# Output products of units 3 and 4 by the seven-for-eight scheme, with the folded weights joined in DRAM

## The chip, the cores and the metric

The kernel runs on one NeuronCore of a Trainium2 chip. The metric is device time in microseconds for one execution. The kernel before takes 518.9 us, the median of 3 runs (518.61 to 520.18). A profiled execution gives a trace of every instruction of the engines: TensorE (PE, with its weight loads as PEld), VectorE (DVE), ScalarE (ACT), GpSimd (POOL) and SyncE (SP, which issues most transfers). All times below are in us.

## The reference

Attention with a local window and block summaries over 4 sequences of 768 tokens (8 heads of 64), then two gates, their product, and two more matrices with no nonlinearity between them:

```python
def _attn_ref(q, k, v):
    B, H, S, D = q.shape                                   # 4, 8, 768, 64
    block, window = (32, 16)
    k_sum = k.reshape(B, H, nb, block, D).max(axis=3)
    v_sum = v.reshape(B, H, nb, block, D).mean(axis=3)
    ...                                                    # scores in the window, and against k_sum
    a = np.exp(scores_all); a = a / (np.sum(a, axis=-1, keepdims=True) + 1e-09)
    return np.matmul(a, np.concatenate([v, v_sum], axis=2))

def _moe_ref(x, w1, w2, w3, w_out):                        # x: 3072 x 512
    a = x @ w1                                             # 512 x 1024
    b = x @ w2
    h = a * b @ w3                                         # 1024 x 1024
    return (h @ w_out)                                     # 1024 x 512
```

Because nothing stands between `w3` and `w_out`, the kernel folds them into one matrix of 1024 x 512, called the folded weights (`wp`).

## The kernel before

**Precision.** Every network matmul is done as three matmuls on values that are split into a rounded high part and a low remainder: high by high, low by high, high by low. ACT casts the high part, DVE subtracts it from the source to get the low part (`low`, L117; `halves`, L569). Tiles with a second index of 2 hold both parts.

**Units.** The 3072 tokens are six units of 512. Units 1 and 2 go through the network in the classic way (`gate`, `project`). Units 3 and 4, and units 5 and 6, go as pairs (n = 1 and n = 2) through block products with seven for eight: both operands are cut into 2 x 2 blocks, seven block products of sums and differences of blocks replace eight, and the results are added up. One product of the gates is 24 matmuls of 128 x 512 (four lanes in four PSUM banks, six each, `lanes`, L633); the gates of a pair are 14 products. The moving operands come from `moving_x` (differences on DVE, casts on ACT, low parts on DVE); the stationary operands come from DRAM as tiles `ws` of 512 KB in a ring of six (`flow_in`). The weights' own sums and differences are formed once by `stationary` and written to DRAM (`wS` for the gates, `pS` for the output).

**Output products.** For units 5 and 6 (`project_fast`, class `Whole`) the output product `h @ wp` is in the same scheme: seven products of 24 matmuls in two lanes with two banks. For units 3 and 4 (`project_split`, class `Split`) it is ordinary: the gates' result is split at once into `hs`, and 192 matmuls `lo` multiply it with the folded weights, loaded from `pW`. The sums of the output weights (`sums_of_output`, L877) load `pW` as tiles `pl`, add the high and low part, and run after the output of units 3 and 4 is issued.

**Order.** The attention works in lumps, one for each of 24 pairs of heads and units; from lump 8 on, `lump(p)` puts the transposes of pair p-2, the scores of pair p, 18 network matmuls, the outputs of pair p-2 and then more network matmuls on TensorE, up to the bound in `UP_TO` (counted in matmul columns). TensorE's order is written out by hand. ACT and DVE follow a written order inside the attention; the remaining work of ACT, DVE, POOL and SP is placed by a planner that simulates the engines by a cost model, with a priority by place in the program and a bonus for what stands in `high_priority`; it often moves work far ahead of its place where its inputs are ready. Each engine then works strictly in that order. `tasks` is a list of background generators (`moving_x`, the sums of weights); `tend` advances the first of them one step for every four matmuls.

Of the kernel before, what the change touches and what calls it, by code (L numbers as in the profile page):

```python
# [19 lines left out]
P = 128  # L20
# [50 lines left out]
def attention_moe(ctx, tc, qG, kW, kT, vP, vW, vB, mask, w1, w2, w3T, wo, out, outT):  # L71
# [41 lines left out]
    pS = {k: [tc.dram_tile([P, 2, 2 * DH], F32, name=f"pS{k}_{c}") for c in range(NF // 4)] for k in range(2, NK - 1)}  # L113
    pW = [tc.dram_tile([P, 2, DO], F32, name=f"pW{i}") for i in range(NF)]
# [324 lines left out]
    def keep_raw(po, u, c):  # L439

        n, half = divmod(u, 2)
        if (n, half) not in raws:
            if half:
                t = sb.tile([P, NC, U], F32, name="xraw", tag="w12", bufs=8)
# [5 lines left out]
        nc.scalar.copy(raws[n, half][c], po[:, :U])  # L450

# [98 lines left out]
    FIRST_OF_GROUP, LAST_OF_GROUP = (0, 2, 4), (1, 3, 6)  # L550

    def source(k, b):


        return b[(0, 1, 0, 1, 0, 0, 1)[k]][(0, 0, 0, 1, 0, 1, 0)[k]]

    def difference(k, b):

        src = source(k, b)
        if k == 2:  # L560
            nc.vector.tensor_tensor(src, b[0][1], src, ALU.subtract)
        elif k == 3:
            nc.vector.tensor_tensor(b[0][1], src, b[0][1], ALU.subtract)
        elif k == 4:
            nc.vector.tensor_tensor(src, b[1][1], src, ALU.subtract)
        elif k == 6:
            nc.vector.tensor_tensor(src, src, b[0][0], ALU.subtract)
# [7 lines left out]
    def moving(k, b, dst):  # L575

        difference(k, b)
        yield 1
        yield from halves(source(k, b), dst)
# [10 lines left out]
    def stationary(load, to_dram, home):  # L590


        t = sb.tile([P, 2, 2, 512], F32, name="wr", tag="ring", bufs=RING)
        yield from load(t)
        a11, a12, a21, a22 = (t[:, i, j] for i in range(2) for j in range(2))
        yield 1

        def finished(k, raw):
# [7 lines left out]
            nc.sync.dma_start(to_dram(k), to.bitcast(F32))  # L606

# [17 lines left out]
    def flow_in(n):  # L625


        while flow and len(ready) < n:
            t = sb.tile([P, 2, 512], F32R, name="ws", tag="x", bufs=6)
            flow.pop(0)(t)  # L630
            ready.append(t)

    def lanes(n, weights_of, moving_of, steps, evacuated, tags, between=None):  # L633

        banks = [ps.tile([P, 512], F32, name="ln", tag=tag, bufs=bufs) for tag, bufs in tags]
        for k in range(NK):
            stationary_of = yield from weights_of(k)
            for i in range(n):
                for c in range(steps):
                    if between and c % KH == 0:  # L640
                        between(k, i * steps // KH + c // KH)
                    a, m = [stationary_of(i, c, w) for w in range(2)], moving_of(k, c)
                    terms = [(a[0], m[0]), (a[1], m[0]), (a[0], m[1])]
                    for j, (x, y) in enumerate(terms):
# [4 lines left out]
                            start=c + j == 0 and k in FIRST_OF_GROUP,  # L649
# [654 lines left out]
```

## Time and profile before

| what | before |
|---|---|
| median of 3 runs | 518.9 us |
| the profiled execution, its time and span | 523.18 and 521.4 us |
| granted TensorE clock, mean | 0.989 |
| busy: PE, DVE, ACT, POOL | 496.7, 368.4, 294.6, 44.4 us |
| moved by DMA | 142.94 MB, mean 274 GB/s |
| matmuls `lo` (output of units 3 and 4) | 192 |
| matmuls `ln<-hT` (output of units 5 and 6) | 168 |

The span is the time from the first to the last instruction; the time of the execution includes what lies around it. Busy times are sums over the span. In the groups, an entry reads: line, engine, operation, what it writes and reads with the shape, its count, its busy time in all and the mean duration of one in ns, and the idle time of the engine just before with what ended it. In the timeline an entry reads: start, duration, engine, line, operation. In the chain of waits an entry is a piece of the path that ended last: start, duration, engine and line. Consecutive operations of DVE and ACT overlap at their ends, so that a row of several is shorter than the sum of their durations.

### The profile page before, as it was taken

Reading aid. Unit: us, or ns where it says so; the run is one execution under the profiler, and the core shown is the slowest. Engines: PE = TensorE matmul, PEld = TensorE weight load, DVE = VectorE, ACT = ScalarE, POOL = GpSimd, SP = SyncE. Lnnn points to the kernel's source line nnn. Section 1 sums busy time; section 2 is a strip of 40 time slices with the busy share of each in tenths; the row PEclk is TensorE's granted clock in tenths of the full one; section 3 lists DMA queues with packets and bytes.
Section 4 is the critical chain, followed back from the end, with each engine's and each line's share of the span. In section 5 each row is a group of like instructions: output and inputs, shape, how many; then the busy total and the mean of one; then the engine's idle time right before and its main releaser. Section 6 shows DMA issues by size and latency. Waiting matters only on the chain.

```text
span 521.4 us, 10271 instructions
## 1 busy us (share of the span) xinstructions
PE 496.7 (95%) x3768; PEld 398.0 (76%) x3768; DVE 368.4 (71%) x877; ACT 294.6 (57%) x839; POOL 44.4 (9%) x78
## 2 busy tenths in 40 slices
PE   1989897999999999999999999999999999999997
PEld 0767676888877777777877778887778888888885
DVE  5989986698644978896668784598444478459982
ACT  5496874467455877778896668448134410401640
POOL 1012725201040000000000000000000000000000
PEclk9989997999999999999999999999999999999999
DMA  8995779999084876869888787666899777556652
GB/s 343 416 406 244 272 248 417 378 410 404 21 298 137 289 292 211 294 237 343 300 300 290 272 294 260 219 216 228 284 370 384 274 284 256 193 196 201 203 183 101
DMA packets 48962, 142.94 MB, mean 274 GB/s; under 512 B 5136, under 2 KB 11792, under 8 KB 46352
## 3 DMA queue, kind: packets, MB, share of 16 engines
q1 hardware_dynamic: 46608, 138.09, 73.2%
q10 hardware_dynamic: 2304, 4.20, 2.1%
q8 instruction: 30, 0.49, 0.4%
q14 instruction: 20, 0.16, 0.1%
HBM read 112.71 MB, written 29.56 MB: 273 GB/s over the span
## 4 chain that ended last, share of the span: by engine, by line
PE 82%; DVE 6%; ACT 6%; DMA 5%; issue 1%; SPq 0%; POOL 0%; POOLq 0%
PE ln L645 37%; PE mm L122 27%; PE lo L122 9%; PE po L430 4%; PE sc L352 3%; ACT sm L380 3%; DMA rows<-in_vP_dram 2%; PE tp L410 2%; DVE wf L185 2%; DMA wraw<-in_w_dram 1%; DVE w L118 1%; DMA wraw<-in_wo_dram 1%; DVE wf L182 1%; DVE sm L366 1%; ACT wf L173 1%
## 5 line engine op out<-in xcount | busy, mean ns | idle before, releaser
L645 PE MATMUL ln<-xT,ws 128*128 128x512 f32 x672 | 156.8, 392 | 0.0
L645 PEld LDWEIGHTS ln<-xT,ws 128*128 128x128 f32 x672 | 125.1, 188 | 27.3 <-issue 1.0
L122 PE MATMUL mm<-x,w 128*128 128x512 f32 x384 | 92.7, 399 | 0.8 <-ACT x L454 0.7
L122 PEld LDWEIGHTS mm<-x,w 128*128 128x128 f32 x384 | 72.3, 191 | 17.8 <-ACT x L454 0.8
L380 ACT ACTIVATE sm<-sm,mx 128x120 f32<-128x120 f32 x192 | 73.7, 387 | 11.6 <-DVE mx L366 11.6
L122 PE MATMUL mm<-w,w 128*128 128x512 f32 x192 | 52.2, 427 | 14.1 <-ACT w L199 11.9
L122 PEld LDWEIGHTS mm<-w,w 128*128 128x128 f32 x192 | 38.1, 204 | 25.0 <-ACT w L199 12.1
L703 DVE TENSOR_TENSOR tmp<-ln,tmp 128x512 f32<-128x512 f32 x64 | 43.7, 689 | 18.5 <-PE ln L645 18.2
L122 PE MATMUL mm<-wp,h 128*128 128x512 f32 x192 | 46.6, 396 | 0.6 <-ACT o L515 0.6
L122 PE MATMUL lo<-ws,hs 128*128 128x512 f32 x192 | 45.5, 394 | 0.0
L366 DVE CUSTOM_DVE_ANT_0 sm<-sc,mask_sb 128x120 f32<-128x120 f32 x192 | 42.0, 277 | 1.9 <-PE sc L352 1.9
L122 PEld LDWEIGHTS mm<-wp,h 128*128 128x128 f32 x192 | 35.3, 188 | 9.1 <-ACT o L515 1.2
L122 PEld LDWEIGHTS lo<-ws,hs 128*128 128x128 f32 x192 | 35.5, 188 | 8.0 <-DVE tmp L703 0.3
L390 ACT ACTIVATE sm<-sm,mx 128x120 f32<-128x120 f32 x128 | 39.0, 386 | 4.5 <-DVE mx L386 4.3
L645 PE MATMUL ln<-hT,ws 128*128 128x512 f32 x168 | 38.2, 389 | 0.0
L571 ACT CAST hT<-hr 128x512 fp32r<-128x512 f32 x28 | 16.9, 623 | 36.3 <-DVE hr L706 27.1
L645 PEld LDWEIGHTS ln<-hT,ws 128*128 128x128 f32 x168 | 31.5, 188 | 6.5
L380 ACT ACTIVATION_READ_ACCUMULATOR sm<-sm,mx 128x1 f32 x192 | 36.5, 190 | 0.0
L430 PEld LDWEIGHTS po<-pt,v 120*64 120x64 f32 x768 | 25.2, 141 | 9.7 <-issue 7.3
L199 ACT CAST w<-wf 128x1024 fp32r<-128x1024 f32 (+1 forms) x22 | 21.3, 966 | 15.9 <-DVE wf L185 15.8
L430 PE MATMUL po<-pt,v 120*64 120x64 f32 x768 | 28.5, 229 | 1.7 <-DVE pt L419 1.6
L118 DVE TENSOR_TENSOR xT<-xraw,xT 128x512 fp32r<-128x512 f32 x28 | 18.5, 686 | 15.8 <-ACT xT L571 15.8
(74 smaller groups left out, 589.0 us busy)
## 6 DMA issues: line engine op xcount, KB each, us to landing
ws<-wS SPq DMA_DIRECT2D x56, 512.0 KB
v<-in_vW_dram SPq DMA_DIRECT2D x24, 512.0 KB
wraw<-in_w3T_dram SPq DMA_DIRECT2D x8, 1024.0 KB
wraw<-in_w_dram SPq DMA_DIRECT2D x8, 1024.0 KB
wS<-sp SPq DMA_DIRECT2D x16, 512.0 KB
ws<-pW SPq DMA_DIRECT2D x16, 512.0 KB
k<-in_kW_dram SPq DMA_DIRECT2D x20, 368.0 KB
raw<-in_kT_dram SPq DMA_DIRECT2D x16, 392.0 KB
```

What stands on the lines that cost most here:

```text
L118: eng.tensor_tensor(dst, src, hi.bitcast(F32), ALU.subtract)
L122: nc.tensor.matmul(acc, lhsT=a, rhs=b, start=first and i == 0, stop=last and i == len(terms) - 1)
L185: nc.vector.scalar_tensor_tensor(out=bits[:, some], in0=words[:, some, 0], scalar=29, in1=bits[:, some], op0=ALU.logical_shift_right, op1= ...
L199: nc.scalar.copy(t[:, 0, some], f[:, some])
L352: nc.tensor.matmul(sc[h][64 * g : 64 * g + 64, i * KR : (i + 1) * KR], lhsT=q[rows, i * P + 64 * g : i * P + 64 * g + 64], rhs=k[rows, i, ...
L366: nc.vector.tensor_tensor_reduce(out=sm[:, j], in0=sc[h][:, i * KR : (i + 1) * KR], in1=mask_sb[:, 0 if blk == 0 else 2 if blk == BLOCKS - ...
L380: nc.scalar.activation(sm[:, j], sm[:, j], AF.Exp, bias=mx[:, 0, j : j + 1], scale=-1.0, accum_out=mx[:, 1, j : j + 1])
L390: nc.scalar.activation(sm[:, j], sm[:, j], AF.Copy, scale=mx[:, 2, j : j + 1])
L430: nc.tensor.matmul(po[cols, at : at + 64], lhsT=v[:KR, g, i, cols], rhs=pt[g][:, (h * NBLK + i) * 64 : (h * NBLK + i + 1) * 64], start=Tru ...
L571: nc.scalar.copy(dst[0], src)
L645: nc.tensor.matmul(banks[i][:, :U], lhsT=x, rhs=y, start=c + j == 0 and k in FIRST_OF_GROUP, stop=c == steps - 1 and j == 2 and k in LAST_ ...
L703: nc.vector.tensor_tensor(to, got, more, ALU.add)
```

## The change

Units 3 and 4 get the same `Whole` class and `project_fast` as units 5 and 6; `Split`, `project_split` and `tile_flow` are gone. What follows from it:

- The order of the seven products becomes a table (`Order`). The gates of units 3 and 4 and both outputs use `LATE`; the gates of units 5 and 6 use `EARLY_SUM`, in which the first four products are copied out by ACT and three are added by DVE. The operands of a product are prepared two products ahead. `moving_x` begins only when the halves that it needs are kept (`kept`).
- The operands `hT` of the output products lie in the buffers `w12` (a pair of tiles per product) instead of `wp`, `wf` and `x`; one half of the raw x of units 5 and 6 moves to the buffers `ring`.
- The folded weights are joined in DRAM: `join_wp` writes the high part of a folded tile to `pR` by SP and then adds the low part onto it with a transfer from POOL's queue (`accum_op=ALU.add`), two tiles in each of lumps 9 to 12. `sums_of_output` loads the joined blocks into four tiles of the `pt` buffers, and needs no additions of its own. `spill_wp` writes only the halves that are still read.
- The sums of the weights are now in a second list, `background`, which `tend` serves when the first list is empty or waits. Those of the output weights are put in at lumps 16 and 18. A load of sums is only issued once they are stored (`stored`).
- In the lumps from 8 on, both halves of the transposed probabilities are copied out by ACT (`evacuate(tp, 'A')`).
- The transposed output `outT` now holds four units; `UP_TO` for lump 17 rises from 2.9 to 3.5 products.

```diff
+    pR = [tc.dram_tile([P, 2, 2, 2 * DH], F32, name=f"pR{c}") for c in range(NF // 4)]
...
+    LATE, EARLY_SUM = (
+        Order(
+            (0, 1, 2, 3, 4, 5, 6),
+            ((0, 1), (2, 3), (4, 5, 6)),
+            {0: (0, 0), 1: (1, 0), 2: (0, 0), 3: (1, 1), 4: (0, 0), 5: (0, 1), 6: (1, 0)},
+            {
+                2: [((0, 0), (0, 1), (0, 0), ALU.subtract)],
+                4: [((0, 0), (1, 1), (0, 0), ALU.subtract)],
+                5: [((0, 1), (1, 1), (0, 1), ALU.subtract)],
+                6: [((1, 0), (1, 0), (0, 0), ALU.subtract)],
+            },
+            {0: (0, None), 1: (2, None), 2: (1, 0), 3: (3, 0), 4: (3, 3), 5: (1, 1), 6: (0, 0)},
+            {5: (1, 3, 1), 6: (0, 2, 0)},
+        ),
+        Order(
+            (0, 4, 5, 6, 2, 3, 1),
...
+            {0: (2, None), 4: (3, None), 5: (1, None), 6: (0, None), 2: (1, 1), 3: (3, 3), 1: (2, 2)},
...
+            {6: (2, 6), 2: ()},
+        ),
+    )
...
-    def stationary(load, to_dram, home):
+    def stationary(name, load, to_dram, home, apart=False):
-        t = sb.tile([P, 2, 2, 512], F32, name="wr", tag="ring", bufs=RING)
+        if apart:
+            t = [[sb.tile([P, 512], F32, name="wr", tag="pt", bufs=6) for _ in range(2)] for _ in range(2)]
...
+            stored.add((name, k))
...
-        while flow and len(ready) < n:
+        while flow and len(ready) < n and (not flow[0][0] or flow[0][0] in stored):
...
+    def add_up(o, k, parts, got):
+        to, more = o.adds[k]
+        if more is None:
+            nc.scalar.copy(parts[to], got)
+        else:
+            nc.vector.tensor_tensor(parts[to], got, parts[more], ALU.add)
...
         def start():
+            while any(kept.get((n, half), 0) < NC for half in range(2 if k > 1 else 1)):
+                yield -1
...
+        def after(self, at, i):
+            if at == 4 and i == 3:
+                tasks.insert(0, staggered(list(self.moving(0))))
+            if at == 6:
+                if i == 0:
+                    for work in self.moving(0):
+                        drain(work)
+                drain(self.moving(1)[i])
...
+                    t = sb.tile([P, 2, 2, U], F32R, name="hT", tag="w12", bufs=8)
...
+        def between(at, j):
             with tc.high_priority(offset=SOONER // 2):
+                if j < 3 and at + 2 < NK:
+                    for work in whole.moving(at + 2):
                         next(work, 0)
+            if n + 1 < NSU and j == 3 and at in (4, 5):
+                moving_x(n + 1, at - 4)
...
     def spill_wp(i):
-        nc.sync.dma_start(pW[i], wp[i].bitcast(F32))
+        n = DO if i >= NF // 2 else DH
+        nc.sync.dma_start(pW[i][:, :, :n], wp[i][:, :, :n].bitcast(F32))
+
+    def join_wp(i):
+        h, c, j = i // (NF // 2), i % (NF // 2) // 2, i % 2
+        to = pR[c][:, :, h, j * DH : (j + 1) * DH]
+        parts = [wp[i][:, w].bitcast(F32).rearrange("p (i d) -> p i d", d=DH) for w in range(2)]
+        nc.sync.dma_start(to, parts[0])
+        nc.gpsimd.dma_start(to, parts[1], accum_op=ALU.add)
...
     def sums_of_output(c):
         def load(t):
-            got = []
             for h in range(2):
-                for j in range(2):
-                    a = sb.tile([P, 2, DO], F32, name="pl", tag="wf", bufs=5)
-                    nc.sync.dma_start(a, pW[h * NF // 2 + 2 * c + j])
-                    got.append((t[:, :, h, j * DH : (j + 1) * DH], a))
-                yield 1
-            for to, a in got:
-                hi, lo = (a[:, w].rearrange("p (i d) -> p i d", d=DH) for w in range(2))
-                nc.vector.tensor_tensor(to, hi, lo, ALU.add)
-                yield 1
-        return stationary(load, lambda k: pS[k][c], {"tag": "v", "bufs": 2})
+                for i in range(2):
+                    nc.sync.dma_start(t[i][h], pR[c][:, i, h])
+            yield from range(1, 5)
+        return stationary("p%d" % c, load, lambda k: pS[k][c], {"tag": "wp", "bufs": NF}, True)
...
-        split = Split()
-        yield from gates(1, split)
-        yield from project_split(1, split)
-        tasks.extend(sums_of_output(c) for c in range(2))
-        whole = Whole(2)
-        yield from gates(2, whole)
-        yield from project_fast(2, whole)
+        for n in range(1, NSU):
+            whole = Whole(n)
+            yield from gates(n, whole)
+            yield from project_fast(n, whole)
...
-    UP_TO[2 * NFIRST + 1] = CLASSIC + 2.9 * FAST
+    UP_TO[2 * NFIRST + 1] = CLASSIC + 3.5 * FAST
...
+    EXTRA.setdefault(16, []).append(lambda: background.append(sums_of_output(0)))
+    EXTRA.setdefault(18, []).append(lambda: background.append(sums_of_output(1)))
+    for i in range(NF):
+        EXTRA.setdefault(9 + i * 4 // NF, []).append(lambda i=i: join_wp(i))
...
-            pt = evacuate(tp)
+            pt = evacuate(tp, 'A')
...
-    first = 4 * TOKENS
+    first = 2 * TOKENS
```

265 lines of the change are left out of this document (115 added, 150 removed).

## The prediction

> **What bounds the kernel now.** I read the page first, for the busy time by engine and the chain that ended last. All times are in us; "product" means one of the seven block products in the seven-for-eight scheme.
>
> ```profile
> span 521.4 us, 10271 instructions
> PE 496.7 (95%) x3768; PEld 398.0 (76%) x3768; DVE 368.4 (71%) x877; ACT 294.6 (57%) x839; POOL 44.4 (9%) x78
> ...
> PE 82%; DVE 6%; ACT 6%; DMA 5%; issue 1%; SPq 0%; POOL 0%; POOLq 0%
> ```
>
> TensorE is busy for 95% of the span and is 82% of the chain, so matmuls are what the time is made of. An average hides stages, so I then cut the span into stages: the classic units 1 and 2 beside the attention, the gates of units 3 and 4, their output products, the gates of units 5 and 6, and their output products. After the window come busy time and count of PE, PEld, DVE, ACT and POOL, then granted clock, DMA share and GB/s.
>
> ```profile
> 86.20:254.40 168.20, 166.47 (x1426) 133.01 (x1424) 123.71 (x343) 113.44 (x360) 17.09 (x31) 0.99 0.78 283
> 254.40:353.70 99.30, 98.74 (x901) 78.87 (x897) 70.61 (x212) 68.04 (x228) 2.85 (x10) 1.00 0.76 261
> 353.70:403.30 49.60, 49.60 (x325) 39.92 (x322) 25.52 (x55) 22.29 (x60) 0.00 (x0) 1.00 0.88 324
> 403.30:479.30 76.00, 76.00 (x337) 62.95 (x336) 49.70 (x77) 15.82 (x29) 0.00 (x0) 1.00 0.68 237
> 479.30:517.60 38.30, 38.27 (x169) 31.36 (x167) 28.64 (x47) 15.93 (x27) 0.00 (x0) 1.00 0.52 174
> ```
>
> From 353.7 on PE has no gap at all, at full clock. In the third stage, the one that the change rewrites, DVE works 25.5 of 49.6 and ACT 22.3. In the last stage, where units 5 and 6 already use the scheme that units 3 and 4 are to get, DVE works 28.6 of 38.3 and PE still doesn't wait. That last stage is the model for what the third becomes. The chain in order of time shows the pace:
>
> ```profile
> 336.74 0.61 PE tp L410 x16
> 337.36 0.98 PE sc L352 x32
> 338.34 4.35 PE ln L645 x18
> 342.68 1.08 PE po L430 x32
> 343.76 8.38 PE ln L645 x36
> ...
> 387.46 15.87 PE lo L122 x69
> 403.33 114.25 PE ln L645 x504
> 517.61 0.69 DVE tmp L842
> ```
>
> The attention comes in lumps: transposes, scores, 18 matmuls of the network, outputs, then some 36 more; its own PE time is 0.61 + 0.98 + 1.08 = 2.67 per lump. Undisturbed, 504 matmuls take 114.25, which is 0.2267 each. The last product ends at 517.61, and DVE and the store to the span's end take 3.8; nothing in the change touches that tail.
>
> **Removed: 24 matmuls.** The groups by shape count them.
>
> ```profile
> L122 PE MATMUL lo<-ws,hs 128*128 128x512 f32 x192 | 45.5, 394 | 0.0
> L645 PE MATMUL ln<-hT,ws 128*128 128x512 f32 x168 | 38.2, 389 | 0.0
> ```
>
> Units 3 and 4 use 192 matmuls for their output; the scheme needs 168. The busy times differ by 7.3, but the 192 are broken up by attention lumps, and these stay. So I price 24 × 0.2267 = **-5.44**.
>
> **Moved: operand work of the output products, now beside the attention.** What units 5 and 6 do in the last stage (28 casts and 4 copies on ACT; 28 low parts, 16 differences and 10 adds on DVE) now also comes once for units 3 and 4, in the products that run beside lumps 22 to 25. In exchange 16 casts and 16 low parts of `hs` and the copies of `o` go. Many such operations run back to back, so their price is the pitch and not the duration:
>
> ```profile
> 490.93 1.89 DVE L118 TENSOR_TENSOR hT<-hr,hT 128x512 fp32r<-128x512 f32 x3
> 400.65 1.14 ACT L571 CAST xT<-xraw 128x512 fp32r<-128x512 f32 x2 [1.58 <-PE lo L122]
> ...
> L366 DVE CUSTOM_DVE_ANT_0 sm<-sc,mask_sb 128x120 f32<-128x120 f32 x192 | 42.0, 277 | 1.9 <-PE sc L352 1.9
> L419 DVE COPY pt<-tp 120x512 f32<-120x512 f32 x22 | 15.1, 686 | 13.8 <-PE tp L410 13.8
> L415 ACT COPY pt<-tp 120x512 f32<-120x512 f32 x24 | 13.8, 581 | 19.1 <-PE tp L410 19.0
> L380 ACT ACTIVATE sm<-sm,mx 128x120 f32<-128x120 f32 x192 | 73.7, 387 | 11.6 <-DVE mx L366 11.6
> L390 ACT ACTIVATE sm<-sm,mx 128x120 f32<-128x120 f32 x128 | 39.0, 386 | 4.5 <-DVE mx L386 4.3
> L450 ACT COPY xraw<-po 128x512 f32<-128x512 f32 x16 | 9.4, 585 | 13.4 <-PE po L430 13.4
> L889 DVE TENSOR_TENSOR wr<-pl 128x512 f32<-128x512 f32 x8 | 5.3, 688 | 7.9 <-DMA pl<-pW 7.9
> ```
>
> On DVE the second and third of the three add (1.89 - 0.69) / 2 = 0.60 each; on ACT the second adds 1.14 - 0.62 = 0.52. A product is 24 × 0.2267 = 5.44 of PE, and with its share of a lump (a lump goes with 2.2 products) 5.44 + 2.67 / 2.2 = 6.65. In lumps 22 and 23 DVE also does eight reductions, at most 8 × 0.28 = 2.2, so 1.0 per product. Product by product, DVE has:
> - last gate product: 4 adds, 4 multiplications, 4 low parts of the second output product and some 3 of the first: 15 × 0.60 + 1.0 = 10.0 against 6.65, so 3.35 behind;
> - output product 1: 4 differences and 4 low parts for product 3, 5.8 against 6.65, 2.5 behind; product 2: 4 low parts, 3.4, caught up;
> - product 3: 4 differences, 4 low parts, 2 adds, 7.0, so 0.35 behind; products 4 and 5 without reductions 6.0 and (with two low parts for unit 5) 7.2 against some 6.2, 1.0 behind; product 6: 2 adds, caught up.
>
> The new code prepares the operands of product i+2 during product i, so each has a whole product (over 5.4) more than it needs, and 3.35 is inside that: **0**. Without that cover it would be 3.35. The adds that empty the two banks are due sooner: a bank is wanted again after the other lane's 12 matmuls, 2.72, less 0.69 for the add, 2.0 spare. They are put 400 places ahead in the order, as the same adds in the last stage are, and there PE never waited.
>
> **Moved: the second half of the transposed probabilities, from DVE to ACT** in lumps 8 to 25. ACT then does two copies in a row, 1.16. The outputs that read them start only after scores and 18 matmuls, 0.98 + 4.35 = 5.33 later: **0**. One row of the timeline speaks against that being free everywhere; the list of waits has no other of PE from 254 to the end:
>
> ```profile
> 307.20 1.04 PE L352 MATMUL sc<-k,q 64*64 64x120 f32 x30 [0.56 <-ACT pt L415]
> ```
>
> There the scores waited for the copy on ACT, behind two `hs` casts that now go. Bounds: -0.56 if it vanishes, 18 × 0.58 = 10.4 if each lump's scores waited for the second copy. I take 0, since it was one lump of 18.
>
> **Added: eight pairs of transfers that join the folded weights,** two pairs in each of lumps 9 to 12: 256 KB written by SP, then 256 KB added on top by a transfer that GpSimd issues once the first has landed. No adding transfer is in the trace. POOL's other work there is to put the key summaries in place, between the keys' landing and the scores:
>
> ```profile
> 197.15 0.38 SPq L319 DMA_DIRECT2D k<-in_kW_dram  x1
> 203.34 1.01 POOL L339 COPY k<-ks 128x96 f32<-128x96 f32 x1 [12.23 <-DMA k<-in_kW_dram]
> 207.17 1.05 PE L352 MATMUL sc<-k,q 64*64 64x120 f32 x32
> 214.68 0.51 POOL L339 COPY k<-ks 128x96 f32<-128x96 f32 x1 [10.32 <-DMA k<-in_kW_dram]
> ```
>
> The 368 KB of keys took 6.2 from issue to landing; POOL idled 10.3 to 12.2 before each copy, and the scores began 2.8 after the copy had ended. A join that waits 6.2 fits into the idle time: **0**. If instead one stands between the landing and the copy in each lump, PE waits 6.2 - 2.8 = 3.4, four times, 13.6. A gain isn't in it. I take 0, nearest to the idle row. Traffic hardly changes: 192 matmuls took 16 loads of 512 KB and the new 168 take 14; eight more loads of 512 KB give way to half as many bytes.
>
> The Trainium skill, page "DMA: Bandwidth & Descriptors", section "Anatomy of one DMA", has an own price for a transfer that GpSimd issues: some 2.0 us plus bytes at 436 thousand per us, an estimate of 2.6 us for 256 KB. By it a join is shorter than 6.2 and the sum keeps its 0; the page's "Rules for kernel authors" also has an accumulating transfer wait for the earlier one, which is the wait that POOL holds. No run here shows either yet.
>
> **Moved: the sums of the output weights,** from beside the output (361 to 429) to beside the gates of units 3 and 4. Eight additions go (5.3 of DVE in all, the row `wr<-pl` above); 8 differences, 8 casts and 8 low parts move into a stage where DVE loses as many `hs` low parts. What counts is that engines work in order and stop for transfers:
>
> ```profile
> DVE wr L889 <- DMA pl<-pW: 7.9, 4, 3.7
> ACT sp L600 <- DMA pS<-sp: 19.3, 4, 9.1
> ```
>
> Where these waits stood before, nothing on DVE was urgent. Beside the gates an add empties one of four banks every 6 matmuls; a bank is due after 18 others, 4.08, less 0.69, 3.4 spare. A wait of 3.7 costs 0.3; two sums, two first waits: **+0.6**. Bounds: 0 if the loads come early, and one wait of the longest kind, 9.1 - 3.4 = 5.7. I take the row of the loads, since the sums' buffers are now eight and not two. Behind such a wait stand the gates' adds, and PE waits for their banks.
>
> **At nothing:** the x of units 5 and 6. Its second product needs the last attention lump's output; counted in products from the start of the gates of units 3 and 4, that is kept at 20.25 and due at 22.0, so 1.75 × 5.44 = 9.5 cover one copy (0.59), two sums, a cast and a low part, under 4. Their banks are copied by ACT in four of seven products, and ACT has 15.8 of 76 there.
>
> **Sum.** -5.44 + 0 + 0 + 0 + 0.6 = -4.84. The profiled execution took 523.18 with a span of 521.4, so 1.78 lies around it: a span of 516.56 and 518.34 for that execution. It was slower than the median of the runs, 518.9; on that the same difference gives **514.1**.
>
> **Rivals.** *More is won*: the wait of 0.56 goes with the `hs` casts and the loads are early: 518.9 - 5.44 - 0.56 = 512.9. For it: nothing else stops PE after 254. Against: the copy itself stays on ACT, with a second behind it. Chance 0.08.
>
> *DVE and ACT fill up beside the attention*: the 3.35 that DVE falls behind is paid, 514.1 + 3.35 = 517.4. For it: in lump 23 ACT has eight exponentials and eight scalings, some 6.2, two copies and one more, 1.7, nine casts at 0.52, 4.7, and an emptied bank or two, 1: 13.6 of 14.6, so little can slip. Against: DVE at 18.07 of 18.70 in a part of the last stage never stopped PE. Chance 0.15.
>
> ```profile
> 479.30:498.00 18.70, 18.70 (x84) 15.48 (x83) 18.07 (x31) 11.56 (x20) 0.00 (x0) 1.00 0.65 207
> ```
>
> *The sums stop an engine beside the gates* by the long row: 518.9 - 5.44 + 5.7 = 519.2, no change. For it the 9.1, against it the number of buffers. Chance 0.10.
>
> *POOL's joins delay the scores, and it gets slower*: place, lumps 9 to 12; price 3.4 each, 514.1 + 13.6 = 527.7, and 520.9 if two of four. It decides from 4.84 / 4 = 1.2 per lump, which is when POOL comes to its copy more than 4.0 after the keys have landed. For it: one in-order queue, and waits of unseen length. Against: 10 idle us per lump. Chance 0.10.
>
> A long stop has its own row:
>
> ```profile
> PE mm L122 <- ACT w L199: 11.9, 2, 11.4
> ...
> 80.00:100.00 20.00, 17.55 (x134) 14.36 (x127) 12.86 (x16) 8.51 (x11) 8.19 (x12) 0.83 1.01 412
> ```
>
> After the stop of 11.4 the granted clock was 0.83 over these 20. The Trainium skill ("TensorE: Matmul & The Clock Gate", "What's actually happening") says that PE falls to half clock after some 3.4 us idle and needs as long to recover; the row agrees, as 17% of 20 is 3.4. By it a stop of 5.7 would cost up to 1.7 more, an estimate, and 519.2 would be 520.9; shorter ones cost only themselves.
>
> **How the numbers follow.** The forecast has 0.57, with an own range of 513.4 to 516. Changes under 0.3% (1.56) can't be told from none: below 517.34 is faster, above 520.46 slower. Faster: 0.57 + 0.08 + half of the second rival, 0.73; no change: the other half and the third, 0.17; slower 0.10. The range goes from 512.7, just under the first rival, to 518.6, over the second; outside lie the slower case and most of the third.
>
> **What would show it.** 168 matmuls `ln<-hT` more and no `lo`; PE without a gap from some 254 to the end, and the last product ending near 512.8. Wrong would be: scores that wait for POOL between 183 and 245; PE waiting for adds or low parts between 330 and 400; a DVE or ACT wait for a joined load longer than 3.4 between 254 and 350.

## The result, and the profile after

The change makes the kernel slower. It takes 536.19 us (median of 4 runs, 534.98 to 537.19) against 519.54 for the kernel before (4 runs, 518.61 to 521.09): a ratio of 1.0316, interval 1.028 to 1.0353, or 16.65 us. The forecast was 514.1.

The page of the changed kernel (busy time by engine), and its waits of TensorE (us in all, times, longest):

```profile
span 533.2 us, 10305 instructions
...
PE 489.5 (92%) x3744; PEld 392.2 (74%) x3744; DVE 364.3 (68%) x881; ACT 315.5 (59%) x881; POOL 51.1 (10%) x86
```

```profile
PE tp L411 <- POOL sm L400: 21.9, 1, 21.9
PE mm L123 <- ACT w L200: 11.9, 2, 11.4
...
```

TensorE is busy for 7.2 us less than before (496.7), as was meant. But one stop of 21.9 is new: the transposes wait for the scaling of a softmax by POOL. The same stop was 0.4 before, and what is left out here is 2.2 or less each. From 190 us on the list has one wait of TensorE left, of 0.2; the stop of 0.56 for a `pt` copy is gone.

Here is where the stop lies, in the timeline of TensorE after (start, duration, engine, line, operation, idle time before and what ended it):

```profile
72.65 5.74 PE L123 MATMUL mm<-w,w 128*128 128x512 f32 x24
100.27 1.11 PE L411 MATMUL tp<-ident,sm 64*120 64x64 f32 x16 [21.88 <-POOL sm L400]
...
105.17 43.87 PE L123 MATMUL mm<-x,w 128*128 128x512 f32 x192
```

The prediction did not look here: 79 to 100 is the end of the weights' folding, long before lump 9. The timeline of POOL shows what stands ahead of the scaling, first of before, then of after:

```profile
74.72 1.15 POOL L339 COPY k<-ks 128x48 f32<-128x48 f32 x2 [9.21 <-DMA k<-in_kW_dram]
76.89 1.79 POOL L399 TENSOR_TENSOR sm<-sm,mx 128x960 f32<-128x960 f32 x1 [1.02 <-DVE mx L386]
```

```profile
65.42 1.21 POOL L878 DMA_DIRECT2D pR<-wp  x1
71.64 1.10 POOL L878 DMA_DIRECT2D pR<-wp  x1 [5.01 <-issue]
82.91 1.09 POOL L878 DMA_DIRECT2D pR<-wp  x1 [10.17 <-issue]
92.45 1.11 POOL L878 DMA_DIRECT2D pR<-wp  x1 [8.45 <-issue]
96.99 1.09 POOL L878 DMA_DIRECT2D pR<-wp  x1 [3.43 <-issue]
97.56 0.90 POOL L340 COPY k<-ks 128x48 f32<-128x48 f32 x2
97.91 2.30 POOL L400 TENSOR_TENSOR sm<-sm,mx 128x960 f32<-128x960 f32 x1
```

Five of the eight joins are not in lumps 9 to 12. The planner put them at 65 to 97, where the folded tiles are ready, ahead of two key copies and the scaling. Between one join and the next POOL stood for 3.4 to 10.2 us, and the releaser of that time is "issue": no semaphore that the profile knows. (In two runs below the third join waits for its plain write until 73 to 76, so up to 3 of the 10.2 may be that.) Behind the last join of the five, the key copies followed at once. The scaling ends at 100.21 instead of 78.68, 21.5 later, which is the stop. While TensorE waits, its clock is halved, and it stays so for most of the first 5 us after (windows of after; after the five engines come the granted clock, the DMA share and GB/s):

```profile
85.00:90.00 5.00, 0.00 (x0) 0.00 (x0) 0.00 (x0) 0.00 (x0) 0.00 (x0) 0.50 1.06 373
90.00:100.00 10.00, 0.00 (x0) 0.00 (x0) 0.00 (x0) 0.00 (x0) 4.12 (x5) 0.50 0.44 66
100.00:105.00 5.00, 4.74 (x110) 4.46 (x112) 2.72 (x3) 2.61 (x3) 4.12 (x8) 0.66 0.21 41
```

Three points on TensorE divide the span: the start of the 192 matmuls `mm<-x` of unit 1, the start of the gates of units 3 and 4, and the start of the last add. For after they are the row at 105.17 above and these two; the rows of before follow:

```profile
272.04 4.42 PE L688 MATMUL ln<-xT,ws 128*128 128x512 f32 x18
```

```profile
529.09 0.69 DVE L708 TENSOR_TENSOR tmp<-ln,tmp 128x512 f32<-128x512 f32 x1 [2.03 <-PE ln L688]
```

```profile
254.42 4.42 PE L645 MATMUL ln<-xT,ws 128*128 128x512 f32 x18
```

```profile
517.61 0.69 DVE L842 TENSOR_TENSOR tmp<-ln,tmp 128x512 f32<-128x512 f32 x1 [2.03 <-PE ln L645]
```

Read in the same way, all kernels of this study compare so (us; "middle" and "last" are lengths, the ratio is to the runs of before on the same chip). A ratio leaves out executions more than 1.5% above the fastest of their kernel: two of five of pool_pt_on_dve, two of 11 of pool_no_lookahead, one of 10 of add_on_dve, and one of 12 of contiguous_in_order, of 1681.4.

| kernel | start of `mm<-x` | middle, to the gates | last, gates to last add | ratio of times, interval |
|---|---|---|---|---|
| before | 86.18 | 168.24 | 263.19 | 1 |
| after | 105.17 | 166.87 | 257.05 | 1.0316 (1.028 to 1.0353) |
| before_plus_joins | 108.00 | 166.58 | 263.21 | 1.0404 (1.0358 to 1.0451) |
| pool_in_order | 85.44 | 171.24 | 257.20 | 1.0022 (1.0 to 1.0044) |
| joins_contiguous | 90.45 | 167.98 | 257.46 | 1.0038 (1.0015 to 1.0061) |
| contiguous_in_order | 84.37 | 172.80 | 257.31 | 1.0003 (0.9973 to 1.0033) |
| same_place_no_adding | 87.86 | 167.95 | 258.01 | 0.9986 (0.996 to 1.0011) |
| pool_plain_transfer | 85.67 | 166.99 | 256.89 | 0.9945 (0.9915 to 0.9976) |
| plain_writes_only | 86.65 | 166.82 | 257.38 | 0.9918 (0.9886 to 0.9951) |
| add_on_pool | 84.13 | 168.07 | 257.54 | 0.9953 (0.9921 to 0.9985) |
| add_on_dve | 86.55 | 169.99 | 259.55 | 0.9964 (0.9929 to 0.9999) |
| pool_no_lookahead | 83.60 | 170.39 | 258.00 | 0.9977 (0.9929 to 1.0024) |
| pool_pt_on_dve | 86.32 | 174.64 | 267.02 | 1.0101 (1.0038 to 1.0165) |

Between the two profiled executions that is 18.99 - 1.37 - 6.14, and 0.32 more behind the last add: 11.80, the difference of the spans (533.2 - 521.4). The medians are 16.65 apart because the profiled execution of before (523.18) is 3.64 above its median and that of after (534.98) 1.21 below.

### The profile page after: what moved, and what is told of

Read it like the earlier page. It is cut to its first block, busy times and chain, and to the rows that moved or that the text cites. A ratio compares the mean times of both kernels' runs of the same rounds, so it can differ in the third digit from the quotient of the medians.

```text
span 533.2 us, 10305 instructions
## 1 busy us (share of the span) xinstructions
PE 489.5 (92%) x3744; PEld 392.2 (74%) x3744; DVE 364.3 (68%) x881; ACT 315.5 (59%) x881; POOL 51.1 (10%) x86
## 4 chain that ended last, share of the span: by engine, by line
PE 79%; DVE 8%; DMA 6%; ACT 4%; issue 2%; POOL 1%; SPq 0%; POOLq 0%
PE ln L688 44%; PE mm L123 25%; PE po L431 4%; PE sc L353 3%; DMA raw<-in_kT_dram 3%; DVE wf L186 3%; PE tp L411 2%; DVE w L119 2%; ACT sm L381 2%; DMA pR<-wp 1%; DVE wf L183 1%; DMA wraw<-in_wo_dram 1%; DMA v<-in_vW_dram 1%; DVE sm L367 1%; ACT w L200 1%
## 5 line engine op out<-in xcount | busy, mean ns | idle before, releaser
L123 PE MATMUL mm<-x,w 128*128 128x512 f32 x384 | 91.1, 394 | 0.9 <-ACT x L457 0.8
L381 ACT ACTIVATE sm<-sm,mx 128x120 f32<-128x120 f32 x192 | 74.0, 389 | 11.4 <-DVE mx L367 11.3
L688 PE MATMUL ln<-hT,ws 128*128 128x512 f32 x336 | 78.3, 392 | 0.0
L688 PEld LDWEIGHTS ln<-hT,ws 128*128 128x128 f32 x336 | 62.6, 188 | 13.4 <-DVE hT L119 0.2
L708 DVE TENSOR_TENSOR tmp<-ln,tmp 128x512 f32<-128x512 f32 x52 | 35.7, 688 | 52.2 <-PE ln L688 38.1
L606 ACT CAST hT<-hr 128x512 fp32r<-128x512 f32 x56 | 32.0, 621 | 43.4 <-DVE hr L765 35.9
L411 PE MATMUL tp<-ident,sm 64*120 64x64 f32 x384 | 17.4, 229 | 22.2 <-POOL sm L400 21.9
L119 DVE TENSOR_TENSOR hT<-hr,hT 128x512 fp32r<-128x512 f32 x56 | 35.7, 687 | 3.1 <-ACT hT L606 3.0
L411 PEld LDWEIGHTS tp<-ident,sm 64*120 64x120 f32 x384 | 13.8, 138 | 31.1 <-POOL sm L400 22.7
L416 ACT COPY pt<-tp 120x512 f32<-120x512 f32 x24 | 13.8, 578 | 37.5 <-PE tp L411 37.5
L340 POOL COPY k<-ks 128x96 f32<-128x96 f32 (+1 forms) x32 | 11.8, 398 | 205.1 <-DMA k<-in_kW_dram 184.5
```

The source lines that it names most:

```text
L119: eng.tensor_tensor(dst, src, hi.bitcast(F32), ALU.subtract)
L123: nc.tensor.matmul(acc, lhsT=a, rhs=b, start=first and i == 0, stop=last and i == len(terms) - 1)
L381: nc.scalar.activation(sm[:, j], sm[:, j], AF.Exp, bias=mx[:, 0, j : j + 1], scale=-1.0, accum_out=mx[:, 1, j : j + 1])
L411: nc.tensor.transpose(to, p, ident[rows, rows])
L606: nc.scalar.copy(dst[0], src)
L688: nc.tensor.matmul(banks[i][:, :U], lhsT=x, rhs=y, start=c + j == 0 and k in o.first, stop=c == steps - 1 and j == 2 and k in o.last, skip ...
```

## The experiments

Two questions were open after the first look: whether the joins alone make the loss, or something else of the change does; and what about a join holds POOL.

**The joins alone, on the kernel before.** The eight pairs of transfers are put into lumps 9 to 12 of the kernel before, and nobody reads what they write.

```diff
+    pR = [tc.dram_tile([P, 2, 2, 2 * DH], F32, name=f"pR{c}") for c in range(NF // 4)]
+    def join_wp(i):
+        ...
+        nc.sync.dma_start(to, parts[0])
+        nc.gpsimd.dma_start(to, parts[1], accum_op=ALU.add)
+    for i in range(NF):
+        EXTRA.setdefault(9 + i * 4 // NF, []).append(lambda i=i: join_wp(i))
```

> The kernel before, with only the eight pairs of join transfers put in at lumps 9 to 12; the joined weights are read by nobody, and the output products stay ordinary. Theory Q: the planner puts the joins as early as in the changed kernel, so the loss of some 17 us appears alone: 535 to 538. Rival B: the same. Rival O: within 1 us of the kernel before.

Measured: 541.18 (541.02 to 543.48), ratio 1.0404. Its waits of TensorE begin with the same line as those of after:

```profile
PE tp L411 <- POOL sm L400: 23.3, 1, 23.3
```

The joins alone cost 20.7 us on a kernel that has none of the other parts. So the loss needs no other part of the change.

**POOL kept in the order of the program.** The planner may no longer move POOL's instructions; the joins then stand at 163 to 215, in lumps 9 to 12 as written.

```diff
-    MANUAL = {engines.PE}
+    MANUAL = {engines.PE, engines.Pool}
```

> The changed kernel with POOL's instructions in their written order from lump 8 on, so that the adding transfers stay in lumps 9 to 12, where the prediction had put them. Nothing is left out. Theory Q (the planner moved five joins to 65-97 us, into POOL's in-order queue ahead of the scaling and the key copies of the last early lumps; PE stood 21.9 us for them): the loss of 17 us goes, what is left is the gain read from the end of the trace (24 matmuls, 5.44, and the 0.56 stop), so about 6 us under the kernel before, ratio 0.988. Rival B (the plain writes, which stay early on SP's queue, and the traffic of the adds fill the DMA engines at 65-90 us): at most half comes back, 527 or more. Rival O (the operand work moved beside the attention costs it): no change, 536.

Measured: 521.01 (519.76 to 523.48). The stop of 21.9 is 1.8, and the start of `mm<-x` is back at 85.44: the place in POOL's queue was the cause of 15 us. But the gain of 6 in the last stage did not show in the total, because the middle stage is now 171.24 instead of 166.87. Its waits of TensorE have two lines that neither before nor after has:

```profile
PE mm L123 <- ACT g L490: 2.4, 1, 2.4
...
PE tp L411 <- ACT xraw L452: 1.6, 1, 1.6
```

ACT came late there, because its next cast had to wait for a store (timeline of ACT, same kernel):

```profile
216.37 0.62 ACT L642 CAST sp<-wr 128x512 fp32r<-128x512 f32 x1 [6.04 <-DMA wS<-sp]
```

So this kernel loses at a second place, by another way. Whether the joins are the cause there is taken up below.

**No adding transfers at all.** The low parts are then missing from the sums for the output products 2 to 5.

```diff
         nc.sync.dma_start(to, parts[0])
-        nc.gpsimd.dma_start(to, parts[1], accum_op=ALU.add)
```

> The changed kernel without the eight adding transfers: the low parts of the folded weights are left out of the sums for products 2 to 5 of the output, so the output is slightly off; the eight plain writes stay as early as they are. Theory Q: about 513, as with POOL in order. Rival B in its form that the plain writes do it: 530 or more. Rival O: 536.

Measured: 516.54 (515.04 to 517.49), ratio 0.9918. The stop of 21.9 is 0.4, the stops of ACT in the middle stage are gone, and the last stage keeps its 257.38. This is what the rest of the change is worth by the runs, about 4 us, where the last stage alone won 263.19 - 257.38 = 5.8. The start differs by 0.5 from before; the middle is 1.4 shorter, but 1.6 of before's is a half clock (its 192 `mm<-x` took 45.47, here 43.89). The two profiled executions are 6.50 apart (523.18 and 516.68), as the stages say; but that of before was 2.74 above the median of its runs on this chip, 520.44, so the medians are only 3.9 apart. The granted clock differs from run to run (last section), which may be the reason; that is not shown.

**Half the rows.** `pR` becomes one tile of 128 rows of 2 KB for each folded tile, so that an adding transfer has 128 rows and not 256 rows of 1 KB. The bytes and the planner's freedom stay. SP's plain write goes to the same tile, and each load of the joined blocks becomes two.

```diff
-    pR = [tc.dram_tile([P, 2, 2, 2 * DH], F32, name=f"pR{c}") for c in range(NF // 4)]
+    pR = [tc.dram_tile([P, DO], F32, name=f"pR{i}") for i in range(NF)]
...
-        nc.gpsimd.dma_start(to, parts[1], accum_op=ALU.add)
+        nc.gpsimd.dma_start(pR[i], wp[i][:, 1].bitcast(F32), accum_op=ALU.add)
...
```

> The changed kernel with one DRAM tile per folded tile, so that a join is 128 rows of 2 KB and not 256 of 1 KB; planned as early as before. Nothing is left out. In the trace POOL stood 5 to 10 us between two joins with no semaphore behind it, about as long as a join takes to land. If the room for descriptors holds it up (half as many descriptors per join), several joins are in flight, POOL comes to the scaling some 15 us sooner, and the time is 518 to 526. If each join waits for the one before it whatever its shape, 534 to 537.

Measured: 522.39 (521.61 to 523.65). The joins are as early as in after, but do not hold POOL (timeline of POOL):

```profile
65.46 1.88 POOL L875 DMA_DIRECT2D pR<-wp  x2
76.05 2.66 POOL L875 DMA_DIRECT2D pR<-wp  x3 [8.71 <-DMA pR<-wp]
78.63 0.67 POOL L340 COPY k<-ks 128x48 f32<-128x48 f32 x2
79.66 1.78 POOL L400 TENSOR_TENSOR sm<-sm,mx 128x960 f32<-128x960 f32 x1 [0.36 <-DVE mx L387]
```

Three adding transfers follow each other in 2.66. What is left is a wait with a semaphore, for the plain write (8.71). One of these lands after 6.6 in the median, so three are under way together, and the theory that only one adding transfer can be falls. What decides is the shape: rows of 2 KB, half as many.

**Is it the rows or the adding?** First the eight transfers wrote the low parts to DRAM of their own, without adding; the low parts are then missing from the sums for products 2 to 5.

```diff
-        nc.gpsimd.dma_start(to, parts[1], accum_op=ALU.add)
+        nc.gpsimd.dma_start(pL[c][:, :, h, j * DH : (j + 1) * DH], parts[1])
```

> The changed kernel with the eight transfers of POOL kept in their place in its queue, with the same 256 rows of 1 KB each, but writing the low parts to DRAM of their own instead of adding them onto the high parts; so the low part of the folded weights is missing from the sums for the output products 2 to 5. Nothing is added in DRAM and POOL doesn't wait for the plain writes. Theory 'rows': a transfer of 256 rows from POOL's queue takes all the room that the queue has, so POOL is held until the one before has landed, whether it adds or not: the eight transfers again stand 4 to 10 us apart, the scaling is late, 528 to 536. Rival 'adding': the hold comes from reading and adding in DRAM; without it the transfers follow each other at about 1.1 us and the time is that of the plain writes alone, 516 to 518.

Measured: 516.85 (515.44 to 518.81), ratio 0.9945. But the place was not kept, as the expectation had assumed: without the wait for the plain write the planner put the transfers at 42 to 83, between other work. That is no clean comparison, so one more run only takes the word that makes them add. The high parts are then overwritten and missing from the sums; the order of the work on POOL, SP, ACT and DVE is that of after.

```diff
-        nc.gpsimd.dma_start(to, parts[1], accum_op=ALU.add)
+        nc.gpsimd.dma_start(to, parts[1])
```

> The changed kernel with one thing taken from it: the eight transfers of POOL write the low part over the high part instead of adding it (so the high part of the folded weights is missing from the sums for the output products 2 to 5). Everything else is as in the changed kernel: the order on every engine, the rows (256 of 1 KB), the waits for the plain writes. In the run before this one the place was another, since the planner moved the transfers to 42 to 83. Theory 'adding': without it five of them in a row at 65 to 97 are issued in some 1 us each once the last plain write has landed, at about 76; the scaling ends near 81, the stop on POOL sm is 3 us or less, and the time is 518 to 521. Theory 'rows': they hold POOL again by 4 to 10 us each, the stop is 15 to 22 us and the time 530 to 536.

Measured: 519.56 (518.05 to 520.05), ratio 0.9986. In the timeline of POOL:

```profile
64.43 1.48 POOL L878 DMA_DIRECT2D pR<-wp  x2
73.26 2.23 POOL L878 DMA_DIRECT2D pR<-wp  x3 [7.35 <-DMA pR<-wp]
77.01 0.39 POOL L340 COPY k<-ks 128x48 f32<-128x48 f32 x2 [1.52 <-DMA k<-in_kW_dram]
77.36 1.79 POOL L400 TENSOR_TENSOR sm<-sm,mx 128x960 f32<-128x960 f32 x1
```

The same five transfers with the same 256 rows in the same place take 0.7 each, and the scaling stands at 77.36. So the hold needs both: a transfer that adds, and 256 rows of 1 KB. The table of DMA queues says what differs (packets, MB, share of 16 engines' span), first after, then joins_contiguous, then same_place_no_adding:

```profile
q0 software_dynamic: 2176, 2.10, 2.8%
```

```profile
q0 software_dynamic: 1152, 2.10, 2.5%
```

```profile
q0 software_dynamic: 640, 2.10, 1.1%
```

Per transfer that is 272, 144 and 80 packets. These counts come out if an adding transfer makes a packet of each row (256 and 128), a plain one of each 4 KB (64), and 16 come on top in all three. A queue with room for 432 packets, but not for 544, and a POOL that waits for that room, would fit all three runs: three transfers of 144 are under way together, and two of 272 do not follow each other at once. The room itself was not measured, so why POOL stands stays open.

**Rows and place together.** Both mends at once (the two diffs above): 128 rows, and POOL in the order of the program.

> Both mends of the adding transfers at once: rows of 2 KB (half the descriptors) and POOL in the order of the program. Theory 'descriptors': what was left in the joins in order (521.0, stops of 2.4 and 1.6 in 205 to 226) comes from 256 rows per transfer; with half of them about 516. Theory 'traffic': the bytes are the same (256 KB written, then 256 KB read and added), so the stops stay and it is 519 to 521.

Measured: 520.66, ratio 1.0003. The middle stage stays long (172.80), and ACT again waits for a store beside which the last joins run (issue of the store by SP, then ACT):

```profile
207.43 0.38 SPq L648 DMA_DIRECT2D wS<-sp  x1
```

```profile
216.85 0.62 ACT L642 CAST sp<-wr 128x512 fp32r<-128x512 f32 x1 [7.54 <-DMA wS<-sp]
```

Half the rows didn't help here, so "descriptors" was wrong. The time fits "traffic", and in 190 to 210 the DMA engines are busy for 0.87 of the time at 217 GB/s, in before for 0.68 at 226. But that the adding makes the store late is not shown by this: the last experiment has the same wait, and stops of the same kind, without an adding transfer.

**A sum in SBUF instead of in DRAM.** POOL adds the two parts into a `pt` buffer, and SP writes the sum once. All is computed, nothing adds in DRAM, and half of the bytes are written.

```diff
-        nc.sync.dma_start(to, parts[0])
-        nc.gpsimd.dma_start(to, parts[1], accum_op=ALU.add)
+        t = sb.tile([P, DO], F32, name="pj", tag="pt", bufs=6)
+        nc.gpsimd.tensor_tensor(t.rearrange("p (i d) -> p i d", d=DH), parts[0], parts[1], ALU.add)
+        nc.sync.dma_start(to, t.rearrange("p (i d) -> p i d", d=DH))
```

> The high and low part of a folded tile are added by POOL into an SBUF tile of the pt buffers, and the sum is written to DRAM once by SP; no adding transfer is left, and half of the bytes of the joins. Everything is still computed. The planner puts the eight additions late by itself (behind the scalings and key copies of the first pairs), because each needs a pt buffer. Theory 'place and traffic' (the adding transfers held POOL early, and where they ran late, in the joins left in order, their traffic made the load of the keys and a store of sums late, 4 us of stops between 205 and 226): with neither left, about 515 to 516.5, like the plain writes alone (516.5); no stop of PE on POOL above 3 us and none on ACT xraw or ACT g. Rival 'POOL shares with DVE': an addition of 128x512 on POOL takes about 1.3 us or more and slows DVE beside it; then 518 or more. Rival 'the rest of the change is only worth 4': no more than 516.5 can be had in any way.

Measured: ratio 0.9953 (0.9921 to 0.9985), 519.68 against 521.54 on that chip, and 515.33 in its best run against 518.28. By the ratio it is faster than before by some 0.5%, and than after by some 3.5%. The expectation's 515 to 516.5 was met only by its best executions, though before was 1.1 longer on this chip, too (521.54 against 520.44); the stops are as it said (2.9 on POOL, none on `xraw`, 0.2 on `g`). Its interval overlaps that of plain_writes_only (0.9886 to 0.9951), so whether the additions on POOL cost anything, as the rival says, stays open. Two additions take 2.5 to 3.0 of POOL, and the planner keeps them at 160 to 207, because each needs a buffer. In ACT's timeline the cast that came at 216.85 above comes at 211.65, after a wait of 1.20:

```profile
211.65 0.62 ACT L642 CAST sp<-wr 128x512 fp32r<-128x512 f32 x1 [1.20 <-DMA wS<-sp]
```

With DVE as the adder instead (`nc.vector.tensor_tensor` in the same place):

> As add_on_pool, but DVE adds the two parts: eight additions of 128x512 at 0.69 each, 5.5 us of DVE between 90 and 215, all still computed. If DVE has room there, the same 515 to 516.5; if DVE sets the pace of the scores in these lumps, up to 5.5 more, 520 to 522.

Measured: 0.9964 (0.9929 to 0.9999). Its interval overlaps that of add_on_pool, so whether DVE is the worse adder isn't settled.

**Two zeros of the prediction, tested on add_on_pool.** First the second half of the transposed probabilities goes back to DVE:

```diff
-            pt = evacuate(tp, 'A')
+            pt = evacuate(tp)
```

> The kernel of add_on_pool with one part of the change undone: in the lumps from 8 on the second half of the transposed probabilities is copied out by DVE again. The prediction's step put its move to ACT at 0 (bounds -0.56 to 10.4). By that step this kernel takes the same as add_on_pool (within 0.6); at equal granted clock the stage from 84 to 252 and the stage from 252 to the end keep their lengths. Rival 'DVE is the fuller engine in 190 to 230' (19.75 of 20 and 18.50 of 20 busy in add_on_pool): 18 copies at 0.60 put back on it cost 2 to 5 us in that stage.

Measured: 1.0101 (1.0038 to 1.0165), against 0.9953 with ACT: 1.5% or some 7.7 us slower (4 to 11 by the two intervals together, an estimate). The profile is of an execution of 533.91, which the ratio leaves out: it shows a place of the loss and not its size, and that the shorter executions wait as long there isn't shown. In it TensorE waits in the first output product (timelines of TensorE and DVE):

```profile
361.56 0.68 PE L411 MATMUL tp<-ident,sm 64*120 64x64 f32 x16
...
374.05 1.76 PE L431 MATMUL po<-pt,v 120*64 120x64 f32 x28 [6.21 <-DVE pt L420]
```

```profile
362.40 5.51 DVE L119 TENSOR_TENSOR hT<-hr,hT 128x512 fp32r<-128x512 f32 x9
367.82 2.49 DVE L602 TENSOR_TENSOR hr<-hr 128x512 f32<-128x512 f32 x4
370.23 2.49 DVE L119 TENSOR_TENSOR hT<-hr,hT 128x512 fp32r<-128x512 f32 x4
...
372.75 0.64 DVE L602 TENSOR_TENSOR hr<-hr 128x512 f32<-128x512 f32 x1
373.31 0.69 DVE L420 COPY pt<-tp 120x512 f32<-120x512 f32 x1
```

The transposes end at 362.2, and the copy starts at 373.31, behind nine low parts, four differences, four more low parts and one more difference. So the rival "DVE is the fuller engine" had the right engine, but this stop is not in the stage that it named, 190 to 230; there the list of waits has 3.3 on `g` of ACT and none on DVE. The loss is probably larger than its 2 to 5.

Then the operands of the output products are prepared one product ahead and not two:

```diff
-                if j < 3 and at + 2 < NK:
-                    for work in whole.moving(at + 2):
+                if j < 3 and 2 <= at + 1 < NK:
+                    for work in whole.moving(at + 1):
```

> The kernel of add_on_pool with the operands of the output products prepared one product ahead instead of two. The prediction's step says that the two products of look-ahead hide 3.35 us of DVE work; without them PE waits for low parts hT between 330 and 400: 3.35 more than add_on_pool, with the waits of PE on DVE hT in the list. Rival 'there is no backlog': the same time and no such waits, so the look-ahead hides nothing.

Measured: 0.9977 (0.9929 to 1.0024), which can't be told from add_on_pool. The order did change: DVE ends the last low part `hT` of these products at 381 and not at 373, of which 1.8 is the later start of the gates. The last stage has 258.00 against 257.54. The list of waits has no line of TensorE on `hT`. So the second product of look-ahead hides nothing that could be seen, and the 3.35 that the prediction priced without it was not there.

The same profile bears on the second cost of pool_in_order. This kernel has no adding transfer and writes half the bytes of the joins, yet ACT waits for a store as there, TensorE stops for ACT (2.3 on `g`, 0.7 on `xraw`), and the middle stage is 170.39:

```profile
213.70 0.62 ACT L642 CAST sp<-wr 128x512 fp32r<-128x512 f32 x1 [5.20 <-DMA wS<-sp]
```

```profile
PE mm L123 <- ACT g L490: 2.3, 1, 2.3
```

In 210 to 230 the DMA engines are busy for 0.98 of the time here and for 0.96 in pool_in_order. In add_on_pool it is 0.99, with a middle stage of 168.07, and in plain_writes_only 0.85, with 166.82. So full DMA engines beside late joins go with these stops, but not every time, and no run takes the adding out of pool_in_order alone. What makes the middle stage longer stays open.

## Why the prediction was wrong, point by point

**The step that failed** is "Added: eight pairs of transfers that join the folded weights", taken at 0 with bounds 0 to 13.6. It cost 18.99 in after, by the start of `mm<-x`, and 20.7 alone. Two assumptions in it were wrong, and a third thing was not seen:

- *Place.* This is the main one. It priced the joins against POOL's idle time in lumps 9 to 12. They run at 65 to 97 and 152 to 162. What the document says of the planner, that it moves work ahead where inputs are ready, was not applied to the new work. The inputs of a join are ready when a folded tile is, so the row to read was POOL's at 60 to 100: there it idled for 9.2 before the two key copies and for 1.0 before the scaling, some 10 in all. The five issues (5.6) and the four gaps between them (27.1) are 22.4 more than that, an estimate from these rows; the scaling ended 21.5 later.
- *Duration.* It took 6.2 from a load of keys. The adding transfers landed after 5.2 in the median, nearly as assumed (the same ones without adding, in same_place_no_adding, after 5.1), but five in a row held POOL one after the other. The Trainium skill's estimate in the prediction (page "DMA: Bandwidth & Descriptors", section "Anatomy of one DMA") was 2.6 for such a transfer; the trace has 5.2, twice as much. Why isn't shown; adding isn't the reason, as the 5.1 says. The row is from the DMA issues of after (the last number is the median from issue to landing):

```profile
pR<-wp POOLq DMA_DIRECT2D x8, 256.0 KB, 5.2
```

- *Traffic.* "Traffic hardly changes" counted bytes. The 2.10 MB of adding transfers take 2.8% of the DMA engines' time, and 1.1% when they don't add. Where they do run in lumps 9 to 12, in pool_in_order, the middle stage is some 4 longer (171.24 against 166.87), behind a store that lands late. That the adding is the reason is not shown, as pool_no_lookahead has 170.39 without it.

**The rival "POOL's joins delay the scores"** had the right side and mechanism, an in-order queue and a wait of unseen length, and was given 0.10. Its place (lumps 9 to 12, four waits of 3.4 each) and its time (527.7) were wrong: one wait of 21.9, on the scaling and not on the scores.

**The removed matmuls** at -5.44 and **the rest of the last stage** were right. After the start of the gates the change wins 263.19 - 257.05 = 6.14, against -4.84 in the sum. The 1.30 more can be put down to the 0.6 for the sums of the output weights, which was not paid, and to 0.56, the stop for the `pt` copy that went; 0.14 is left. This is the rival "more is won", in this stage. DVE waited for the joined loads 2.3 at most, and was full for 20 us without stopping TensorE (windows of after):

```profile
360.00:380.00 20.00, 20.00 (x182) 16.01 (x181) 20.00 (x46) 13.62 (x37) 0.49 (x1) 1.00 0.90 313
```

**The copy moved to ACT at 0** was right as a price of the move. But the move is not neutral: undone, the kernel takes some 7.7 us more. The step looked for what ACT would suffer and not for what DVE was spared.

**The operand work at 0 with a cover of 3.35:** the 0 was right, the cover was not needed. TensorE needs nothing urgent from DVE there, once the `pt` copy is gone from it.

**One reading of the trace was wrong.** The prediction put the stop of 11.4 ahead of the clock of 0.83 in 80 to 100. That stop is the first 11.4 us of the program. The half clock of before lies at 83 to 90, and follows the stop of 2.4 on POOL's key copy (timeline of TensorE, then windows):

```profile
83.26 1.08 PE L352 MATMUL sc<-k,q 64*64 64x120 f32 x16 [2.44 <-POOL k L339]
```

```profile
82.00:84.00 2.00, 0.74 (x16) 0.70 (x16) 2.00 (x3) 1.94 (x2) 0.69 (x2) 0.72 1.04 434
84.00:88.00 4.00, 4.00 (x44) 3.28 (x37) 2.28 (x4) 0.84 (x2) 0.02 (x1) 0.50 1.01 406
88.00:90.00 2.00, 2.00 (x7) 1.55 (x6) 0.89 (x2) 1.05 (x1) 1.88 (x4) 0.58 1.07 415
```

These windows make 1.1 + 4.0 + 1.7 = 6.8 at half clock. The 3.4, which is 17% of 20, is the time that was lost by it and not the time that it lasted, and the stop ahead of it is shorter than 3.4. So the row does not agree with 3.4 of idling and 3.4 to recover, as the prediction said; only the price of its third rival hung on that.

## What to carry to other kernels

Where a planner may move work, price a new transfer at the earliest place at which its inputs are ready, and look at what stands behind it there on the issuing engine; the place in the program says nothing. The sum in DRAM by adding transfers was dear here on three counts (the issuing engine held, DMA time per byte, a wait for the first write), and an add in SBUF with one plain write gave a kernel that is 0.5% faster than before. When a step is put at nothing because an engine has room, ask also what the move has freed on the engine that it left.

## What the runs showed of the hardware

- Between two adding transfers of 256 KB with rows of 1 KB, POOL stood for 3.4 to 10.2 us, with no semaphore behind it (six gaps in after). With rows of 2 KB, or without adding, they followed each other at 0.7 to 0.9.
- An adding transfer made 272 packets with 256 rows and 144 with 128, a plain one from the same queue 80. For the same 2.10 MB the DMA engines took 2.8%, 2.5% and 1.1% of the span.
- After a stop of under 3 us the clock was halved in one run, and not in another. The two pairs of rows are the same scores and the windows 78 to 90, first of add_on_pool, then of add_on_dve; the granted clock was 1.00 and 0.72:

```profile
82.48 0.64 PE L353 MATMUL sc<-k,q 64*64 64x120 f32 x16 [2.91 <-POOL k L340]
```

```profile
78.00:90.00 12.00, 9.09 (x128) 7.54 (x125) 9.42 (x12) 7.11 (x9) 5.56 (x7) 1.00 1.02 413
```

```profile
83.64 1.08 PE L353 MATMUL sc<-k,q 64*64 64x120 f32 x16 [2.95 <-POOL k L340]
```

```profile
78.00:90.00 12.00, 8.68 (x122) 7.02 (x121) 7.45 (x9) 5.76 (x7) 4.99 (x7) 0.72 0.99 400
```

The runs of one kernel differ with the mean clock: add_on_pool took 515.33 at a mean clock of 1.0 and 522.99 at 0.989, and before 518.70 at 1.0 and 523.44 at 0.990. The Trainium skill ("TensorE: Matmul & The Clock Gate", "What's actually happening") says that the clock goes by a window of some 3.4 us that runs freely and doesn't start anew with the kernel. That would let the same stop fall into one window or be cut by the border of two. The rows fit it, but show no windows; and as both stops are shorter than 3.4, the sparse work beside them would have to count as idle, which no run here shows. The 515.33 and 522.99 of one kernel are 1.5% apart, so a difference of 1% between such kernels needs many runs.
